# Retention with SiLU feed-forward on one core: two products moved into visits 7 and 9, with the order of loads, slices and read-backs around them

## The chip, the core and the metric

The kernel runs on one core of one Trainium2 chip. Its engines are TensorE (PE, with weight loads listed as PEld), VectorE (DVE), ScalarE (ACT), GpSimd (POOL) and SyncE (SP), which here issues the DMAs. The metric is the device time in microseconds: the kernel before took 631.07 us as the median of 6 runs (629.87 to 632.33).

## What is computed

```python
# q, k, v: (4, 8, 768, 64) float32        attention without softmax, one decay for each head
gamma = 1.0 - 2.0 ** (-5.0 - np.arange(H))
for t in range(S):
    state = gamma * state + einsum('bhd,bhe->bhde', k[:, :, t], v[:, :, t])
    y[:, :, t] = scale * einsum('bhd,bhde->bhe', q[:, :, t], state)
x = y.transpose(0, 2, 1, 3).reshape(3072, 512)
h = x @ w_in                               # w_in  (512, 2048)
g = h * (1.0 / (1.0 + np.exp(-h)))
out = g @ w_out                            # w_out (2048, 512)
```

The weights come as 64-bit numbers, so each slice of them has to be converted before it is used.

## The kernel before

**Units.** The sequence is cut into NC = 6 chunks of 128 steps. A unit is one chunk of one of the B = 4 batches; there are 24, numbered chunk by chunk, so units 0 to 3 make chunk 0 and units 4 to 7 chunk 1. For a unit, PE transposes k and q (`stage_t`, called T), multiplies k with v and k with q (`stage_s` and `stage_a`, the score step SC), and later forms the unit's output y (`stage_y`) in two halves: the masked scores and the products with the state of one half of the heads (YA), then those of the other half (YB). Between the two halves `fence` makes PE wait for a memset on POOL that waits for PE's last matmul of the first half. DVE multiplies the scores with the decay mask (`am`, L462), forms `mid` and the new state (L470, L474) and scales q (L395). ACT copies PSUM tiles out: kt and qt (L430), and the output y (`ys`, L531). Each y becomes three parts of x, high, low and third (`split_x`, called X: L544 on ACT, L547 and L550 on DVE).

**Weights.** w_in has NF = 16 slices of 128 columns. A slice is loaded by three DMAs (`load_w`), converted (`convert_steps`: L197 on ACT; L200, L203, L207, L210, L213 and L218 on DVE), and split in three parts (`split_steps`: L121 and L127 on ACT, L124 and L129 on DVE). There are two buffers (tag "wf") for slices as they come in; `convert_w(i)` asks for the load of slice i + 2, which has to wait until slice i has been read. `begin_w` does the conversion of the next slice, `end_w` its split. `take_w` does both behind a given product. The 16 slices of w_out are converted by `take_w` in the course of chunks 0 to 5, written to DRAM, and read back and split during chunk 5 (`get_w`, `w_out`, two ahead).

**Products.** `product_in(c, f)` is one product of the first feed-forward step: chunk c with slice f, 12 matmuls of 128 by 512. Eight of them go to a PSUM tile ha (parts 0 and 1) and four to hb (part 2). `close_in` copies ha (ACT L644), subtracts hb (DVE L648) and applies SiLU (ACT L652). The result g goes to DRAM (`put_g`), because the second step, g times w_out (L886), begins only after all 96 products. PSUM tiles for products and transposes rotate over three banks (`turn`).

**What sets the order.** PE's order is as written in the program. Up to `early_order.close()` (L793) the order of the other engines is as written too: it is a list of the steps T, K, SC, A, Q, YA, YB, X and W for units 0 to 5. After that the compiler's scheduler orders SP, ACT, DVE and POOL, within the bounds of `issue_after`, which puts instructions of an engine behind a given one on that engine (`taken_out` is the last subtraction L648, `masked` the last mask L462, `evac` the last copy of qt, `held` the last high part of x).

**Visits.** From unit 6 on the work is done in visits. `visit(m)` transposes unit m, does the score step of unit m - 1 and the output of unit m - 2, asks for loads of units m + 1 and m + 2, and then ends and begins slices. `halves(m)` is a visit that stops once, before the score step, so that a product can be placed there. With EARLY = 8, visits 6, 7, 8 and 9 come first; visit 8 holds product (0,2). Visits 10, 11 and 12 are taken in halves, with a product behind each half (`pairs`); visit 13 follows the last of the pairs. Then come groups of three products (`three`), and visits 14 to 25 are strewn among the later products (`at`). Chunk c = 1 can be multiplied only after visit 9, which finishes unit 7.

Begun slices before the change: `begin_w` runs in visits 6, 8, 10, 11, 12 and 13 (slices 2 to 7), and `end_w` in the next visit each time.

Of the kernel before, what the change touches and what calls it, by code (L numbers as in the profile page):

```python
# [13 lines left out]
FP32 = mybir.dt.float32  # L14
# [19 lines left out]
def kernel(  # L34
# [29 lines left out]
    B, H, S, D = q.shape  # L64
    DM, DF = moe_w_in.shape
# [15 lines left out]
    def pool(name, bufs, **kw):  # L81
        return ctx.enter_context(tc.tile_pool(name=name, bufs=bufs, **kw))
# [6 lines left out]
    one = pool("one", 1)  # L89
    hpool = pool("hpool", 3)  # L90
    stage = pool("stage", 2)
# [40 lines left out]
    def split_w(*of):  # L132
        steps = split_steps(*of)
        next(steps)
        yield
        list(steps)
# [4 lines left out]
    EARLY = 2 * B  # L141
# [79 lines left out]
    def convert_w(i):  # L221

        if i + W_AHEAD not in staged:
            load_w(i + W_AHEAD)
        out = []
        steps = convert_steps(i, out)
        for _ in range(6):
            next(steps, None)

        def rounded():  # L230
            list(steps)
            return out[0]

        return rounded
# [40 lines left out]
    def begin_w():  # L275

        i = taken[0]
        taken[0] += 1
        split = split_w(i, convert_w(i)(), "wi", scale, w_sb, True)
        next(split)  # L280
        half_split.append(split)
# [61 lines left out]
    behind_next, behind_copy, half_split = [], [], []  # L343
    taken_out, copied, masked, fenced = [], [], [], []
# [76 lines left out]
    def stage_t(n):  # L421

        for name, to, bufs, src, tp in (
                ("kt", kt, 2, kqv["k"][n], turn(f"kp_{n}")),
                ("qt", qt, 3, kqv["q"].pop(n), banks("q", f"qp_{n}", 1)[:, 0])):
            tp = tp.rearrange("p (a t) -> p a t", a=HP)
            for a in range(HP):
                nc.tensor.transpose(tp[:, a, :], src[:, 2 * a : 2 * a + 2, :], ident)
            to[n] = one.tile([128, HP, C], FP32, tag=name, name=f"{name}_{n}", bufs=bufs)
            evac[:] = [nc.scalar.copy(out=to[n], in_=tp).ins]  # L430

    def score_tile(n):
        u = banks("s", f"sc_{n}")
        sc, sums = (u[:, :, ts(i, 4 * D)].rearrange("p o (a t) -> p o a t", a=HP)
                    for i in range(2))
        return sc, sums

    def stage_s(n, sums):

        kf, vs = kqv["k"].pop(n), kqv["v"][n]  # L440
        for a in range(HP):
            for o in range(2 if units[n][0] < NC - 1 else 1):
                for j in range(2):
                    nc.tensor.matmul(sums[ts(j, D), o, a, :], lhsT=kf[ts(o, D), 2 * a + j, :],  # L444
                                     rhs=vs[ts(o, D), 2 * a + j, :], start=True, stop=True,
                                     skip_group_check=True)

    def stage_a(n, sc):

        ktn = kt.pop(n)  # L450
        for a in range(HP):
            for o in range(2):
                for j in range(2):
                    nc.tensor.matmul(sc[ts(o, D), j, a, :], lhsT=ktn[ts(j, D), a, ts(o, D)],  # L454
                                     rhs=qt[n][ts(j, D), a, ts(o, D)], start=True, stop=True,
                                     skip_group_check=True)
# [62 lines left out]
    def finish_y(n, yp):  # L519
        list(steps_y(n, yp))  # L520
# [60 lines left out]
    def visit(m):  # L581

        list(halves(m))

    def halves(m):

        first, mid, last = (0 <= m - i < len(units) for i in range(3))
        if first and m < FAR:
            stage_t(m)
        if last:  # L590
            scores, states_with, yp = stage_y(m - 2)
            scores()
            states_with(0)
        yield
        if mid:
            sc, sums = score_tile(m - 1)
            stage_s(m - 1, sums)
            stage_a(m - 1, sc)
            if 1 < m <= 3 * B + 1 and units[m - 1][1] == 0:
                next_chunk()  # L600

            with tc.issue_after(taken_out[0]) if m > 3 * B + 1 else ExitStack():
                finish_a(m - 1, sc, sums)
            scale_q(m - 1)
            if m > 3 * B + 1 and units[m - 1][1] == B - 1:

                behind_copy.append(next_chunk)
        if first and m < FAR:
            scale_k(m)
        if last:  # L610
            states_with(1)
            finish_y(m - 2, yp)

        if FAR <= m < len(units):
            with tc.issue_after(fenced[0]):
                part_t(m)
        for name in "kqv":
            for n in (m + 1, m + 2):
                if n >= EARLY and n == (m + 1 if name == "v" or n > FAR else m + 2):
                    load(name, n)  # L620
        if EARLY - 2 <= m < 3 * B + 2:
            with tc.issue_after(masked[0]):
                end_w()
                if m not in (EARLY - 1, EARLY + 1):
                    begin_w()


# [2 lines left out]
    def product_in(c, f):  # L630
        close_in(c, f, *multiply(c, f))
# [23 lines left out]
    def put_g(keep):  # L655
        while len(pending) > keep:
            c, f, g = pending.pop(0)
            nc.sync.dma_start(out=g_dram[c, f], in_=g)
# [14 lines left out]

    def get_w(f):
        if f < NF:
            t = stage.tile([128, DM], FP32, tag="wf", name=f"wr_{f}")
            nc.sync.dma_start(out=t, in_=wo_dram[f])
            w_got[f] = t

    def w_out(f):  # L680
        list(split_w(f, w_got.pop(f), "wo", 1.0, wo))
        get_w(f + 2)

    blocks = {}

    def split(n):
        if n >= len(order):
            return
        c, f = order[n]
        get(n + G_AHEAD)  # L690
        g = got.pop(n)
# [9 lines left out]
        ready[n] = t  # L701

    G_AHEAD = 4
    S_AHEAD = 3


# [5 lines left out]
    def SC(n):  # L712
        sa[n] = sc, sums = score_tile(n)
        stage_s(n, sums)
        stage_a(n, sc)
        asteps[n] = steps_a(n, sc, sums)

    def A(n):
        next(asteps[n], None)

    def YA(n):
        ys[n] = stage_y(n)
        ys[n][0]()
        ys[n][1](0)

    def YB(n):
        ys[n][1](1)
        ysteps[n] = steps_y(n, ys[n][2])

    def X(n):  # L730
        next(ysteps[n], None)
# [3 lines left out]
    def W(i, times=1):  # L735
        if i not in slices:
            slices[i] = early_slice(i)
        for _ in range(times):
            next(slices[i], None)
# [5 lines left out]
    K, Q = scale_k, scale_q  # L745
# [20 lines left out]
    YB(1), X(1), X(1)  # L766
    T(3), K(3)
    X(1), X(1)
    YA(2), SC(3)
    A(3), A(3), Q(3), A(3)  # L770
    YB(2), X(2), X(2)
    W(1), W(1)
    X(2), X(2)
    YA(3), YB(3), X(3), X(3)
    W(1)
# [18 lines left out]

    product_in(0, 1)
    put_g(1)
    visit(EARLY - 2)
    visit(EARLY - 1)
    eighth = halves(EARLY)
    next(eighth)  # L800
    product_in(0, 2)
    put_g(1)
    list(eighth)
    visit(EARLY + 1)
    half_visits = (x for m in range(EARLY + 2, 3 * B + 1) for x in chain(halves(m), (None,)))
    next(half_visits)

    half = NF // 2
    pairs = [(1, 0), (1, 1), (1, 2), (0, 3), (1, 3), (0, 4)]
    three = [(1, 4)] + [x for f in range(5, half) for x in ((0, f), (1, f), (2, f - 5))]  # L810
    rest = ([(2, f) for f in range(half - 5, half)] +
            [(c, f) for c in range(2) for f in range(half, NF - 4)])
    last = ([(c, f) for c in range(2) for f in range(NF - 4, NF)] +
# [8 lines left out]
    takes += [(4, f) for f in (3, 7, 11, 14)]  # L822
    takes += [(5, f) for f in (1, 3, 5)]
    behind = {x: lambda: next(half_visits) for x in pairs[:-1]}
    behind[0, 4] = lambda: [visit(3 * B + 1), behind_next.append(end_w)]
    at = ([(1, NF - 1)] + [(2, f) for f in range(NF - 7, NF - 2, 2)] +
          [(c, 4 * i + 1) for c in range(3, NC - 1) for i in range(B)])
    for i, x in enumerate(at):
# [9 lines left out]
    for n, (c, f) in enumerate(steps):  # L838
        if n - 2 in far:
            behind_next.append(lambda m=far[n - 2]: scale_k(m))  # L840
        if n - 3 in far:
            behind_copy.append(lambda m=far[n - 3]: [join_t(name, m) for name in "qk"])
        product_in(c, f)
        if (c, f) in takes:
            take_w(taken_out[0], n < len(pairs + three))
        put_g(1)
        behind.get((c, f), lambda: None)()
        if n - 1 in far:
            turn_t(far[n - 1])
        if c == NC - 1:  # L850
            if f == 0:
                get_w(0)
                get_w(1)
            if f < NF - 4:
                w_out(f)
            if f >= NF - 6:
                if f == NF - 6:
                    for n in range(G_AHEAD):
                        get(n)
                if f >= NF - S_AHEAD:  # L860
                    split(f - NF + S_AHEAD)
    put_g(0)

    for c in range(NC):
# [9 lines left out]
        for f in range(NF):  # L874
            n = c * NF + f
            split(n + S_AHEAD)
            if n < 4:
                w_out(NF - 4 + n)
            t = ready[n]
# [17 lines left out]
        for b in range(B):  # L897
            oa, ob = acc[b]
            o = one.tile([128, DM], FP32, tag=("kt", "qt")[b % 2], name=f"o_{c}_{b}",
                         bufs=(2, 3)[b % 2])  # L900
# [45 lines left out]
```

## Time and profile before

| | |
|---|---|
| median of 6 runs | 631.07 us (629.87 to 632.33) |
| the profiled execution | 631.8 us, its span 629.8 us |
| mean granted TensorE clock | 0.992 |
| PE busy | 606.1 us, 96% of the span |
| DVE busy | 422.7 us, 67% |
| ACT busy | 319.0 us, 51% |
| DMA | 107.31 MB, mean 170 GB/s |
| first matmul | at 4.29 us |
| product (1,0) begins | at 65.21 us |
| the second feed-forward step begins | at 362.72 us |

Times are counted from the first instruction of the profiled execution. A row of the time-ordered view gives the start, the time, the engine, the line, the operation with its tiles, and in brackets how long the engine had been idle and what ended that. A row of the waits view gives the waiting engine and line, what it waited for, the sum, the number and the longest. A busy time is a share of one engine alone; that an engine is busy doesn't say that the end depends on it.

### The profile page before, as it was taken

What the parts mean: (1) busy time and instruction counts of PE and PEld (TensorE: products, weight loads), DVE (VectorE), ACT (ScalarE), POOL (GpSimd) and SP (SyncE); (2) the same over time, 40 slices, a digit from 0 to 9 for tenths busy, and PEclk for the clock granted to TensorE, in tenths of its full rate; (3) what the DMA queues carried; (4) which work ended last, traced back from release to release, by engine and by line L of the source; (5) the groups of instructions that cost most, each with busy time, mean ns of one, the idle gap of its engine ahead of it and who ended that gap; (6) DMA issues with size and microseconds to landing.
All of it is one profiled execution on the core that took longest, in us unless ns stands there. A gap on an engine that the chain in (4) does not pass through costs nothing.

```text
span 629.8 us, 13488 instructions
## 1 busy us (share of the span) xinstructions
PE 606.1 (96%) x5384; PEld 498.3 (79%) x5384; DVE 422.7 (67%) x729; ACT 319.0 (51%) x611; POOL 22.6 (4%) x79
## 2 busy tenths in 40 slices
PE   5797999999999999999999999999999999999997
PEld 4675787888888888888887878888888888888886
DVE  4778798788979887777598885463645545554631
ACT  7578797666756566566567871221412221322311
POOL 3000000000000121111000000000000000000000
PEclk9799999999999999999999999999999999999999
DMA  9997687445578799998657764342433524442301
GB/s 189 214 228 179 164 242 234 151 153 181 161 218 235 203 265 245 239 248 243 240 195 234 221 191 134 103 160 72 148 120 93 175 70 131 134 120 81 134 1 67
DMA packets 137998, 107.31 MB, mean 170 GB/s; under 512 B 94800, under 2 KB 103248, under 8 KB 137936
## 3 DMA queue, kind: packets, MB, share of 16 engines
q1 hardware_dynamic: 135056, 101.21, 56.7%
q10 hardware_dynamic: 2880, 5.24, 2.2%
q8 instruction: 42, 0.69, 0.5%
q14 instruction: 20, 0.16, 0.1%
HBM read 66.06 MB, written 36.70 MB: 163 GB/s over the span
## 4 chain that ended last, share of the span: by engine, by line
PE 85%; DVE 5%; SPq 4%; DMA 3%; ACT 2%; issue 1%; DVEq 0%; POOLq 0%
PE ha L637 25%; PE o L886 20%; PE oa L886 14%; PE hb L637 12%; PE ob L886 7%; SPq L159 3%; PE y L493 3%; PE sc L444 1%; PE sc L454 1%; DMA kqv<-in_q_dram 1%; DMA wr<-wod 1%; DVE g L648 1%; DVE ca L213 1%; DMA wf<-in_moe_w_in_dram 1%; DVE cs L207 1%
## 5 line engine op out<-in xcount | busy, mean ns | idle before, releaser
L637 PE MATMUL ha<-xt,wi 128*128 128x512 f32 x768 | 194.8, 395 | 2.3 <-DVE g L648 1.5
L637 PEld LDWEIGHTS ha<-xt,wi 128*128 128x128 f32 x768 | 143.0, 189 | 34.9 <-DVE g L648 2.8
L886 PE MATMUL o<-wo,gs 128*128 128x512 f32 x564 | 143.2, 389 | 0.0
L886 PEld LDWEIGHTS o<-wo,gs 128*128 128x128 f32 x564 | 105.9, 188 | 21.9
L697 DVE TENSOR_TENSOR gs<-gr,gs 128x512 fp32r<-128x512 f32 x96 | 62.2, 686 | 88.5 <-ACT gs L695 88.5
L695 ACT ACTIVATE gs<-gr 128x512 fp32r<-128x512 f32 x96 | 53.5, 621 | 131.5 <-issue 130.8
L886 PE MATMUL oa<-wo,gs 128*128 128x512 f32 x376 | 115.9, 389 | 0.3 <-DVE g L648 0.3
L637 PE MATMUL hb<-xt,wi 128*128 128x512 f32 x384 | 103.0, 390 | 0.1
L648 DVE TENSOR_TENSOR g<-g,hb 128x512 f32<-128x512 f32 x96 | 65.7, 684 | 46.4 <-ACT g L644 28.4
L652 ACT ACTIVATE g<-g 128x512 f32<-128x512 f32 x96 | 60.5, 630 | 53.3 <-DVE g L648 53.2
L637 PEld LDWEIGHTS hb<-xt,wi 128*128 128x128 f32 x384 | 71.9, 188 | 15.8 <-DVE wi L129 0.6
L886 PEld LDWEIGHTS oa<-wo,gs 128*128 128x128 f32 x376 | 70.5, 188 | 15.2 <-DVE g L648 0.7
L886 PE MATMUL ob<-wo,gs 128*128 128x512 f32 x188 | 73.8, 393 | 0.3 <-ACT g L644 0.3
L644 ACT ACTIVATE g<-ha 128x512 f32<-128x512 f32 x96 | 56.8, 592 | 29.6 <-PE ha L637 20.9
L698 DVE SCALAR_TENSOR_TENSOR gs<-gs 128x512 fp32r<-128x512 f32 x96 | 62.1, 685 | 0.0
L886 PEld LDWEIGHTS ob<-wo,gs 128*128 128x128 f32 x188 | 35.3, 188 | 9.4 <-DVE o L904 1.6
L197 ACT ACTIVATE ca<-wf 128x512 f32<-128x512 f32 x32 | 21.4, 670 | 8.2 <-DVE cw L218 6.7
L462 DVE TENSOR_TENSOR am<-sc,decay 128x512 f32<-128x512 f32 x24 | 16.5, 688 | 11.2 <-PE sc L454 11.2
L213 DVE SCALAR_TENSOR_TENSOR ca<-wf,ca 128x512 f32<-128x512 uint32 x32 | 22.7, 710 | 0.4
L903 ACT ACTIVATE o<-o 128x512 f32<-128x512 f32 x10 | 6.0, 598 | 33.4 <-PE o L886 33.0
L207 DVE SCALAR_TENSOR_TENSOR cs<-ca,cs 128x512 uint32<-128x512 uint32 x32 | 22.1, 690 | 0.8
L493 PE MATMUL y<-qt,mid 64*64 64x64 f32 x384 | 21.0, 227 | 0.6 <-POOL token L365 0.6
(91 smaller groups left out, 566.3 us busy)
## 6 DMA issues: line engine op xcount, KB each, us to landing
gd<-g SPq DMA_DIRECT2D x96, 256.0 KB, 3.1
gr<-gd SPq DMA_DIRECT2D x96, 256.0 KB, 2.7
wf<-in_moe_w_out_dram SPq DMA_DIRECT2D x16, 512.0 KB, 4.2
out_dram<-o ACTq DMA_DIRECT2D x20, 256.0 KB, 2.1
wf<-in_moe_w_in_dram SPq DMA_DIRECT2D x16, 256.0 KB, 4.1
wf<-in_moe_w_in_dram SPq DMA_DIRECT2D x32, 128.0 KB, 3.9
kf<-in_k_dram SPq DMA_DIRECT2D x16, 256.0 KB, 5.1
qf<-in_q_dram SPq DMA_DIRECT2D x16, 256.0 KB, 4.6
```

The source lines that it names most:

```text
L197: nc.scalar.activation(out=a.bitcast(FP32), in_=hi.bitcast(FP32), func=AF.Abs, scale=65536.0)
L207: nc.vector.scalar_tensor_tensor(out=s, in0=a, scalar=3, in1=s, op0=ALU.logical_shift_left, op1=ALU.bitwise_or)
L213: nc.vector.scalar_tensor_tensor(out=p.bitcast(FP32), in0=lo, scalar=2.0 ** -52, in1=p.bitcast(FP32), op0=ALU.mult, op1=ALU.mult)
L493: i = nc.tensor.matmul(yp[ts(e, D), o, a, :], lhsT=lhsT, rhs=rhs, start=(e, o) not in started, stop=True, skip_group_check=True).ins
L637: nc.tensor.matmul(hb if i == 2 else ha, lhsT=w_sb[f][:, i, ts(kk, 128)], rhs=xt[c][:, i, kk, :], start=kk == 0 and i != 1, stop=kk == KIN ...
L644: copied[:] = [nc.scalar.activation(out=hs, in_=ha, func=AF.Copy, scale=ONE_E).ins]
L648: taken_out[:] = [nc.vector.tensor_tensor(out=hs, in0=hs, in1=hb, op=ALU.subtract).ins]
L652: nc.scalar.activation(out=hs, in_=hs, func=AF.Silu)
L695: nc.scalar.activation(out=t[:, 0, :], in_=g, func=AF.Copy, scale=HALF)
L697: nc.vector.tensor_tensor(out=t[:, 1, :], in0=g, in1=high, op=ALU.subtract)
L698: nc.vector.scalar_tensor_tensor(out=t[:, 2, :], in0=t[:, 1, :].bitcast(FP32), scalar=-1.0 / EPS, in1=high, op0=ALU.mult, op1=ALU.add)
L886: nc.tensor.matmul(o, lhsT=g, rhs=wo[f][:, i, :], start=f == 0 and i != 1, stop=f == NF - 1 and i != 0)
```

## The change

Four things are done. The early list puts the second half of unit 2's output, and the first step of X(2) (the copy of y), ahead of unit 3's score step. Visits 7 and 9 are taken in halves with products (0,2) and (0,3) inside; visit 8 has none, and `pairs` takes up (1,4) from the front of `three` where it has lost (0,3). The slices are begun sooner: slice 2 before visit 6, behind the subtraction of (0,1), and slices 3 to 7 in visits 7, 9, 10, 11 and 12. And the read-backs of w_out use the five buffers of tags kt and qt instead of the two of "wf", and run four ahead instead of two.

```diff
@@ visit
             with tc.issue_after(masked[0]):
                 end_w()
-                if m not in (EARLY - 1, EARLY + 1):
+                if m not in (EARLY - 2, EARLY, 3 * B + 1):
                     begin_w()
@@ get_w, w_out
-            t = stage.tile([128, DM], FP32, tag="wf", name=f"wr_{f}")
+            tag = "kqkqq"[f % 5]
+            t = one.tile([128, DM], FP32, tag=f"{tag}t", name=f"wr_{f}",
+                         bufs=2 if tag == "k" else 3)
...
-        get_w(f + 2)
+        get_w(f + W_READ)
...
+    W_READ = 4
@@ the early list
-    YA(2), SC(3)
-    A(3), A(3), Q(3), A(3)
-    YB(2), X(2), X(2)
-    W(1), W(1)
+    YA(2), YB(2), X(2)
+    SC(3), A(3), A(3), Q(3), A(3)
+    X(2), W(1), W(1)
     X(2), X(2)
@@ the visits
+    with tc.issue_after(taken_out[0]):
+        begin_w()
     visit(EARLY - 2)
-    visit(EARLY - 1)
-    eighth = halves(EARLY)
-    next(eighth)
-    product_in(0, 2)
-    put_g(1)
-    list(eighth)
-    visit(EARLY + 1)
+    for m, f in (EARLY - 1, 2), (EARLY, None), (EARLY + 1, 3):
+        parts = halves(m)
+        next(parts)
+        if f:
+            product_in(0, f)
+            put_g(1)
+        list(parts)
...
-    pairs = [(1, 0), (1, 1), (1, 2), (0, 3), (1, 3), (0, 4)]
-    three = [(1, 4)] + [x for f in range(5, half) for x in ((0, f), (1, f), (2, f - 5))]
+    pairs = [(1, 0), (1, 1), (1, 2), (1, 3), (0, 4), (1, 4)]
+    three = [x for f in range(5, half) for x in ((0, f), (1, f), (2, f - 5))]
...
-    behind[0, 4] = lambda: [visit(3 * B + 1), behind_next.append(end_w)]
+    behind[pairs[-1]] = lambda: [visit(3 * B + 1), behind_next.append(end_w)]
@@ chunk 5
-                get_w(0)
-                get_w(1)
+                for i in range(W_READ):
+                    get_w(i)
```

## The prediction

> **What bounds the kernel now.** I read the page first: parts 1 and 2.
>
> ```profile
> PE 606.1 (96%) x5384; PEld 498.3 (79%) x5384; DVE 422.7 (67%) x729; ACT 319.0 (51%) x611; POOL 22.6 (4%) x79
> ...
> PE   5797999999999999999999999999999999999997
> ```
>
> PE is idle for 629.8 - 606.1 = 23.7 us in all, and the change leaves PE's work alone. So it can only earn from idle time, or from work done at a low clock. The slices show where idle time is: in the first seven slices (to about 110 us), and hardly after. The second view is the engines' busy time by stage: visits 6 to 9 (39 to 65.2 us), the pairs of products (69.9 to 94), the step from pairs to threes (94 to 105).
>
> ```profile
> 39.00:65.20 26.20, 20.13 (x616) 16.58 (x616) 20.52 (x40) 22.62 (x61) 0.35 (x4) 1.00 0.79 196
> ...
> 69.90:94.00 24.10, 23.93 (x475) 19.80 (x468) 22.05 (x43) 20.94 (x51) 0.27 (x3) 1.00 0.78 217
> 94.00:105.00 11.00, 10.14 (x53) 7.40 (x45) 10.73 (x20) 8.69 (x21) 0.00 (x0) 1.00 0.81 230
> ```
>
> After the length the columns are PE, PEld, DVE, ACT, POOL, clock, DMA share, GB/s. In the visits PE has 6.07 us free, DVE 5.68, ACT only 3.58. In the pairs PE is full. At the step DVE is full (10.73 of 11.00) and PE loses 0.86. Third, who PE waits for from 36 to 105 us:
>
> ```profile
> PE y L493 <- issue: 1.6, 2, 1.5
> PE y L493 <- DVE qt L395: 1.5, 2, 0.7
> PE y L493 <- DVE am L462: 1.0, 1, 1.0
> PE ha L637 <- DVE g L648: 0.9, 2, 0.7
> PE ha L637 <- ACT wi L127: 0.8, 2, 0.6
> ```
>
> These are chains, not one engine: the scores of a unit go to DVE for the mask (am) and for the scaling of q (qt), and PE needs both for the unit's output. A product of 12 matmuls placed between is what PE could do meanwhile. Fourth, DVE in time order shows that it too waits there, before the mask of unit 5:
>
> ```profile
> 42.89 0.69 DVE L462 TENSOR_TENSOR am<-sc,decay 128x512 f32<-128x512 f32 x1 [1.94 <-PE sc L454]
> ```
>
> Last, the clock around unit 3, by stretches of 3.41 us:
>
> ```profile
> 18.79:22.20 3.41, 1.30 (x51) 1.15 (x54) 3.02 (x6) 2.55 (x5) 0.00 (x0) 1.00 0.69 180
> 22.20:25.61 3.41, 2.24 (x80) 2.05 (x72) 1.27 (x3) 0.65 (x2) 0.09 (x1) 0.50 0.96 205
> 25.61:29.03 3.42, 2.88 (x51) 2.57 (x52) 2.23 (x5) 1.99 (x4) 0.09 (x1) 0.50 1.13 228
> 29.03:32.44 3.41, 3.41 (x12) 2.92 (x12) 2.83 (x5) 2.87 (x8) 0.00 (x0) 0.50 0.97 227
> ```
>
> From 22.20 to 32.44 PE ran at half clock, after a stretch in which it was busy for 1.30 of 3.41 us (it waited for unit 3's q).
>
> **Part 1: unit 2's output ahead of unit 3's scores.** Before, unit 3's output waits 1.44 us and starts at 25.87, because the copy of unit 2's output (ACT L531) comes at 25.23, behind the mask and mid of unit 3. With YB(2) and X(2) first, that copy can run at about 23, under SC(3). The cost: the two halves of unit 2's output now follow each other, and the fence between them (a POOL memset) is bare; where it is bare in this stage PE waits 0.28 and 0.30. So SC(3) ends at about 24.5 instead of 24.2, the mask at 25.2, and unit 3's output starts at 25.2: 0.65 earlier, so product (0,0) starts at 29.3 instead of 29.95. No DMA moves in this part: SP issues only loads here, in unchanged order.
>
> [...] By the row alone the part is worth 0.65. [...] I take 0.3. Bounds: 0, and 1.3 if the clock rises one window earlier (below).
>
> **Part 2: products in visits 7 and 9.** Before, only visit 8 holds a product, (0,2), and pairs hold (0,3). Afterwards (0,2) stands in visit 7 and (0,3) in visit 9, visit 8 has none, and one product less is left behind the visits. A product takes 1.81 + 0.91 = 2.72 us (the chain of waits, 106.93 to 109.65).
>
> The budget for the same 26.2 us: PE 20.13 + 2.72 = 22.9; DVE 20.52 + 0.60 (one more subtraction, L648, start to start) = 21.1, or 24.0 if slice 4's conversion also falls before (1,0) (six operations, 2.9 start to start); ACT 22.62 + 0.5 + 0.6 (copy L644, silu L652) + 0.57 (L197) = 24.3. It fits, with ACT the tightest at 93%.
>
> The chain, by hand. Slice 2's conversion moves to right behind the subtraction of (0,1), DVE 40.9 to 43.8. Of these 2.9 us, 1.94 fill the wait shown above; the other 0.9 is queued ahead of unit 5's mask, which comes at 43.8 instead of 42.9. ACT's L197 moves from 43.75 into its 0.90 idle before 40.35, and the copy of unit 4's output comes about as much earlier; PE gets to unit 5's scores part at 44.5 (44.94 before), and through its states when q is scaled, 45.7. Slice 2's split (L121, L124, L127, L129: 0.6 each) follows unit 4's xh and ends near 48.0, against 54.2 before. So (0,2) starts at about 46 and ends at 49.4, with 0.9 of waits inside. SC(6) is queued behind it on PE: 49.4 instead of 45.69, and unit 6's mask 50.4 instead of 49.27. This is the new wait of the change; behind it stand unit 6's output and visit 8. Visit 8, now free of a product, catches up: unit 7's mask about 55.5 (57.01 before), since slice 3's conversion, 2.9, is in DVE's queue ahead of it. Then (0,3) from 57.6 to 61.6, again with about 1 us of waits for its slice, unit 8's mask 62.6 (62.55 before), and (1,0) starts at 64.8 to 65.6, where it starts at 65.21 before with a product less behind it. I take 0.4 later than before: gain 2.72 - 0.4 = 2.3. Bounds: 1.0 if ACT must keep its 3.58 us free (1.7 of added work lengthens the stage), 3.7 if the hand timeline is all cover; below nothing only by the rival further on.
>
> The 1.5 us "issue" wait, at 46.81 inside visit 7, falls with the product ahead of it into time that PE spends multiplying; I count no gain for it, because DVE was then busy to 51.7 anyway. SP: slice 4's load now waits for slice 2's conversion at 43 instead of 49 (SP's longest wait, 3.9 us). If it is queued ahead of unit 8's k and q loads, these land at about 50 instead of 45; unit 8 is transposed at about 50.7, so this costs nothing, but with little to spare. POOL only does fences.
>
> **Part 3: the step to threes.** With conversions begun one visit sooner, the last is done in visit 12 and visit 13 only ends one: 2.9 us less for DVE just before 94 to 105, where PE loses 0.86 behind DVE's subtractions. I take 0.8; bounds 0 and 1.1.
>
> **Part 4: w_out read back four ahead.** Before, the read-backs share two buffers with the incoming w_out slices: the first is issued at 328.92 although product (5,0) began at 318, and ten reads wait on SP for DVE L124, 12.6 us in all. PE feels little of it: 0.68 at 335.37 (DVE L648) and 0.27 + 0.34 at 365, where ACT had stood 0.48 for a read: 1.29 together. Five kt/qt buffers are free by then, the last visit lying in (4,13), and are free again before the first output tiles. The four reads at (5,0) put four issues of 0.32 ahead of one write of g on SP; a write later by 1.3 us is covered by three buffers at 2.72 us a product. I take 0.6; bounds -0.3 and 1.3.
>
> **Sum.** 0.3 + 2.3 + 0.8 + 0.6 = 4.0. The profiled execution took 631.8 (span 629.8 and 2.0 around it), so 627.8 there; it lies 0.7 above the median 631.07, so 627.1 for the median. From (1,0) on, PE is full, so nothing should give it back.
>
> **Rivals.**
> 1. DVE and ACT set the visits. The product gets in, but the visits grow by most of it: part 2 gives 0.5, part 3 0.4, the others 0.9 as above. For: ACT is 93% full in the budget. Against: the new work goes into waits that the trace shows. 631.07 - 1.8 = 629.3. Chance 0.17.
> 2. The clock falls in visit 8. [...] Half clock for one or two stretches around (0,3) costs 1 to 2.5: about 628.8. [...] Chance 0.13.
> 3. The clock rises one window sooner. The stretch 25.61 to 29.03 held 2.88 busy and did not raise it; without 0.26 of its wait it holds 3.1. From 5.13 to 8.55 PE was busy 3.3, and its matmuls were fast from then. If it rises at 29.03, part 1 gives 1.3: 626.1. Chance 0.15.
> 4. Slower: (0,2) stops PE in visit 7. If the queues of DVE and ACT put slice 2's work behind visit 6's, as they do now, it is ready at 54.2, and SC(6) with everything behind it stands until (0,2) ends at 55.7 instead of 49.4. That costs 6.3 against 4.0: 633.4. It decides for slower from slice 2 landing 4 us behind my 48.0. Against: the conversion is written ahead of visit 6 and tied to the subtraction of (0,1). Chance 0.1.
>
> The forecast itself: 0.45.
>
> **Numbers.** About 0.2% (1.3 us) is what a measurement of this kernel can tell from no change: faster is below 629.8. Forecast, rival 3, most of rivals 2 and 1 lie there: 0.77. Within: 0.13. Slower: 0.10. Range 624.9 (the upper bounds of two parts together) to 630.6 (rival 1 with parts 3 and 4 at their low bounds); rival 4 stays outside.
>
> **What would show it.** Right: (0,2) starts near 46 and (0,3) near 57.6; (1,0) near 65; DVE's 1.94 wait filled; PE busy about 23 of 26.2 in the visits; no wait of 0.7 for L648 near 98 or 335; copy L531 of unit 2 near 23; the clock up at 32.4. Wrong: PE waiting over 2 us for L127 in visit 7 (rival 4), a half clock near 56 (rival 2), (1,0) past 67 (rival 1), or new PE waits in the pairs.

## The result and the profile after

The changed kernel takes 627.3 us (median of 21 runs, 625.77 to 630.84) against 631.26 us before (42 runs). The ratio is 0.994, with a 95% interval of 0.9926 to 0.9954, so it is faster by 2.9 to 4.7 us, 3.8 in the middle. The forecast was 627.1. The profiled execution took 626.11 us, its span 624.3. Page of the changed kernel, parts 1 and 2:

```profile
PE 606.0 (97%) x5384; PEld 497.5 (80%) x5384; DVE 422.4 (68%) x729; ACT 317.4 (51%) x611; POOL 22.1 (4%) x79
...
PE   6888999999999999999999999999999999999997
...
PEclk9999999999999999999999999999999999999999
```

PE's work is the same, and the early slices are fuller. But the last row shows a trap: in this execution the clock never dropped after the start, while the profiled execution of before ran at half clock from 22.20 to 32.44 us. The two spans therefore differ by 5.5 us, more than the medians (4.0), and the early stage can't be compared between them. What can be compared are stretches in which both ran at full clock. Who PE waited for from 36 to 105 us, after:

```profile
PE y L493 <- DVE am L462: 1.4, 2, 0.8
PE ha L637 <- ACT wi L127: 1.2, 2, 0.6
PE sc L454 <- issue: 1.1, 1, 1.1
PE y L493 <- DVE qt L395: 0.7, 1, 0.7
PE hb L637 <- ACT g L644: 0.5, 1, 0.5
PE ha L637 <- DVE g L648: 0.4, 1, 0.4
```

The waits did not vanish: these lines sum to 5.3 us, those of before to 7.1 (5.8 in the five shown there, 1.3 in three shorter ones). What changed is what PE gets done between them. The stretch from unit 6's transposes to product (1,0), in the order length, PE, PEld, DVE, ACT, POOL, clock, DMA; first before, then after:

```profile
39.99:65.21 25.22, 19.15 (x613) 15.81 (x611) 20.02 (x39) 22.18 (x60) 0.35 (x4) 1.00 0.78 192
```

```profile
36.90:63.57 26.67, 22.04 (x625) 17.63 (x623) 22.00 (x42) 23.25 (x61) 0.35 (x4) 1.00 0.88 212
```

It holds 12 matmuls more (x625 to x613), one product of 2.72 us by the prediction's row, and is 1.45 longer: 1.27 gained. DVE in time order shows slice 2's conversion right behind the subtraction of (0,1), and unit 5's mask behind it without a wait, where 1.94 stood before:

```profile
37.17 0.69 DVE L648 TENSOR_TENSOR g<-g,hb 128x512 f32<-128x512 f32 x1 [0.75 <-PE kp L428]
37.77 0.42 DVE L200 TENSOR_SCALAR cs<-wf 128x512 uint32<-128x512 uint32 x1
...
40.48 0.69 DVE L218 TENSOR_TENSOR cs<-cs,ca 128x512 f32<-128x512 f32 x1
41.09 0.68 DVE L462 TENSOR_TENSOR am<-sc,decay 128x512 f32<-128x512 f32 x1
```

Two more stretches can be cut in every trace: from (1,0) to (2,0), which holds the step to threes, and from the last bare fence of the products (312.24 before, 307.28 after) to the end, which holds the read-backs and the second feed-forward step. PE's waits at the step to threes, where (2,0) begins with the last row of each view (103.92 before, 98.94 after):

```profile
100.58 2.11 PE L637 MATMUL ha<-xt,wi 128*128 128x512 f32 x8 [0.68 <-DVE g L648]
103.92 2.11 PE L637 MATMUL ha<-xt,wi 128*128 128x512 f32 x8 [0.18 <-DVE g L648]
```

```profile
97.37 1.20 PE L637 MATMUL hb<-xt,wi 128*128 128x512 f32 x4 [0.50 <-ACT g L644]
98.94 2.11 PE L637 MATMUL ha<-xt,wi 128*128 128x512 f32 x8 [0.37 <-DVE g L648]
```

All stretches are differences of starts in PE's time-ordered view.

| kernel | median us | unit 6 to (1,0) | (1,0) to (2,0) | last fence to end |
|---|---|---|---|---|
| before | 631.26 | 25.22 | 38.71 | 317.56 |
| changed | 627.3 | 26.67 | 35.37 | 317.02 |
| order alone | 631.41 | 25.21 | 38.72 | 317.62 |
| visits and slices alone | 628.02 | 26.65 | 35.08 | 317.75 |
| read-backs alone | 630.24 | 26.18 * | 40.10 * | 316.97 |
| slices sooner alone | 630.06 | 27.69 * | 37.88 | 318.63 |
| slice 2 late | 635.12 | 32.85 * | 35.08 | 316.96 |
| split not held | 626.94 | 26.40 | 35.11 | 317.41 |
| read-backs two ahead | 627.67 | 26.66 | 35.17 | 316.95 |
| no scaling of k | 625.76 | 26.68 | 35.09 | 317.11 |
| no scaling of q | 625.05 | 25.18 | 35.05 | 317.09 |
| useless work in visits 7, 8 | 633.71 | 25.68 | 39.22 | 318.06 |
| work in the wait for q | 626.95 | 26.67 | 35.08 | 317.04 |
| split and two ahead | 625.7 | 26.40 | 35.09 | 316.98 |

A star marks an execution whose clock was halved inside the stretch. Kernels with (0,3) inside the visits have one product of 2.72 more in the first stretch and one less in the second. Between them, from (2,0) to that fence, both kernels took the same: 208.32 before and 208.34 after.

Each execution in the experiments, and each of the changed kernel's, is also recorded with its mean granted clock. A least-squares fit over these, with one offset for each kernel and one common slope on (1 - clock) x 630 us, gives 0.57 us of time for each us of clock lost and a scatter of 0.73. One execution of before, at 681.48 us with a clock of 0.852, was slow as no other and is left out. Differences at equal clock below are differences of these offsets, with their 95% interval: the changed kernel is 2.65 +- 0.34 faster than before. The runs were taken in several series, and the kernel before alone lies 0.15 above its common offset in one of them and 0.16 and 0.20 below it in two others, so a difference between kernels of different series is uncertain by some 0.3 more.

### The profile page after: what moved, and what is told of

The parts are those of the page before. It is cut to its first block, busy times and chain, and to the rows that moved or that the text cites. A ratio compares the mean times of both kernels' runs of the same rounds, so it can differ in the third digit from the quotient of the medians.

```text
span 624.3 us, 13508 instructions
## 1 busy us (share of the span) xinstructions
PE 606.0 (97%) x5384; PEld 497.5 (80%) x5384; DVE 422.4 (68%) x729; ACT 317.4 (51%) x611; POOL 22.1 (4%) x79
## 4 chain that ended last, share of the span: by engine, by line
PE 89%; DVE 7%; issue 1%; ACT 1%; DMA 1%; POOL 0%; DVEq 0%; POOLq 0%
PE ha L637 26%; PE o L890 20%; PE oa L890 14%; PE hb L637 13%; PE ob L890 7%; PE y L493 4%; PE sc L444 2%; PE sc L454 2%; PE kp L428 1%; PE qp L428 1%; DVE am L462 1%; DVE cs L207 1%; DMA wf<-in_moe_w_out_dram 1%; DVE ca L213 1%; DVE wol L124 0%
## 5 line engine op out<-in xcount | busy, mean ns | idle before, releaser
L648 DVE TENSOR_TENSOR g<-g,hb 128x512 f32<-128x512 f32 x96 | 65.7, 684 | 49.9 <-ACT g L644 29.2
L644 ACT ACTIVATE g<-ha 128x512 f32<-128x512 f32 x96 | 56.9, 593 | 32.9 <-PE ha L637 19.0
L462 DVE TENSOR_TENSOR am<-sc,decay 128x512 f32<-128x512 f32 x24 | 16.5, 687 | 6.4 <-PE sc L454 6.2
```

The costliest lines, as they stand in the source:

```text
L462: mask = nc.vector.tensor_tensor(out=am[n], in0=sc, in1=decay, op=ALU.mult).ins
L644: copied[:] = [nc.scalar.activation(out=hs, in_=ha, func=AF.Copy, scale=ONE_E).ins]
L648: taken_out[:] = [nc.vector.tensor_tensor(out=hs, in0=hs, in1=hb, op=ALU.subtract).ins]
```

## The experiments

**Part 1 alone.**

```diff
-    YA(2), SC(3)
-    A(3), A(3), Q(3), A(3)
-    YB(2), X(2), X(2)
-    W(1), W(1)
+    YA(2), YB(2), X(2)
+    SC(3), A(3), A(3), Q(3), A(3)
+    X(2), W(1), W(1)
```

> Only part 1: unit 2's second half and its copy ahead of unit 3's scores; all else as before. Theory A (read from the two traces): the profiled pair differs by 3.1 us up to visit 6, more than the 0.3 that the prediction gave part 1, but most of that is the half clock, which fell in one execution and not in the other; the order itself is worth 0.3 to 1.3: 630.0 to 631.0. Rival B: the order is the largest part of the gain, 2 us or more: under 629.3. Both expect the copy of unit 2's output near 23 us, no wait of 1.4 us for it, and everything from visit 6 to the end as long as before.

Measured: 631.41 us (14 runs), ratio 1.0004 (0.9984 to 1.0025); at equal clock 0.24 +- 0.41 faster. Its profiled execution also ran at half clock in the stretches 22.20 to 32.44, as before's did, so the two can be laid side by side. Time-ordered views of this kernel, of ACT, DVE and PE:

```profile
23.08 0.58 ACT L531 COPY ys<-y 128x512 f32<-128x512 f32 x1 [1.55 <-PE y L493]
```

```profile
24.82 0.69 DVE L462 TENSOR_TENSOR am<-sc,decay 128x512 f32<-128x512 f32 x1 [2.80 <-PE sc L454]
```

```profile
25.66 1.13 PE L493 MATMUL y<-am,kqv 64*64 64x64 f32 x32 [0.92 <-DVE am L462]
...
29.75 1.63 PE L637 MATMUL ha<-xt,wi 128*128 128x512 f32 x3
```

The copy comes at 23.08 as foreseen, and unit 3's output waits 0.92 instead of 1.44. But the scores end later. From the first state products of unit 2 to the mask it is 3.16 us (21.66 to 24.82) against 2.23 before (22.00 to 24.23): at half clock the bare fence and the second half cost 0.9. A head start of 0.34 hides a part of that: the load of unit 3's q stopped PE for 0.85 in this execution, not for 2.11. Unit 3's output and product (0,0) start 0.2 sooner (29.95 before); at unit 6 0.07 of it is left (39.92 against 39.99). In this pair the order is worth nothing.

At full clock it is worth more. From the first half of unit 2's output to that of unit 3 it is 4.02 us in the old order (slices sooner alone, 21.24 to 25.26) and 3.51 in the new one (the changed kernel, 21.29 to 24.80), 0.5 gained. Up to unit 6 the old order took 15.97 there, and the four executions of the new one that were at full clock 15.61 to 16.02. So the order gives 0 to 0.4 in single executions. Over all runs its effect can't be told from none, nor from the predicted 0.3. Rival B, the order as the main part, falls.

**Parts 2 and 3 alone**: the changed kernel with the early list and the read-backs as before.

> Parts 2 and 3 alone: products in visits 7 and 9, slices begun sooner, the early list and the read-backs as before. Theory A (the traces): from unit 6's transposes to product (1,0) 26.7 us instead of 25.2 with one product of 2.72 more, so 1.3 gained; from (1,0) to (2,0) 0.6 gained; 1.9 in all: 629.4. The prediction's own sizes give 2.3 + 0.8 = 3.1: 628.2. Rival B (the early order is the main part) would leave under 1: over 630.3.

Measured: 628.02 us (14 runs), ratio 0.9946 (0.9928 to 0.9964), at equal clock 2.13 +- 0.41 faster. Rival B falls. The stretches give what theory A expected, 25.22 + 2.72 - 26.65 = 1.3 and 38.71 - 2.72 - 35.08 = 0.9, but the median moved by 2.9, nearer the prediction's 3.1. The difference is mostly clock: the mean granted clock of these runs is 0.9966, before's 0.9946, which the fit prices at 0.7.

**Part 4 alone** (`W_READ = 4` is set as in the change, and chunk 5 begins with four reads).

```diff
-            t = stage.tile([128, DM], FP32, tag="wf", name=f"wr_{f}")
+            tag = "kqkqq"[f % 5]
+            t = one.tile([128, DM], FP32, tag=f"{tag}t", name=f"wr_{f}",
+                         bufs=2 if tag == "k" else 3)
-        get_w(f + 2)
+        get_w(f + W_READ)
...
+    W_READ = 4
```

> Part 4 alone: w_out read back four ahead in the kt and qt buffers. Theory A (the traces): chunk 5's products take 0.7 longer, the second feed-forward step 1.2 less; 0.5 gained: 630.8, hard to tell from no change in time, but both halves show in the trace. Rival: the 0.7 longer stems from the other parts (another position of visits against the read-backs), then this kernel gains 1.2: 630.1.

Measured: 630.24 us (22 runs), ratio 0.9983 (0.9969 to 0.9996); at equal clock 0.59 +- 0.34 faster, and the stretch from the last fence to the end 0.59 shorter. PE's waits in it besides the fence's own, this kernel's only one and then the three of before:

```profile
341.86 2.11 PE L637 MATMUL ha<-xt,wi 128*128 128x512 f32 x8 [0.40 <-DVE g L648]
```

```profile
335.37 2.12 PE L637 MATMUL ha<-xt,wi 128*128 128x512 f32 x8 [0.68 <-DVE g L648]
...
364.96 0.50 PE L886 MATMUL ob<-wo,gs 128*128 128x512 f32 x1 [0.27 <-ACT g L644]
365.80 0.73 PE L886 MATMUL oa<-wo,gs 128*128 128x512 f32 x2 [0.34 <-DVE g L648]
```

From fence to second step it is 51.13 against 50.48, 0.65 longer, and the rest is 1.24 shorter: theory A in both halves. More split work falls into the first part (DVE does 75 operations there instead of 72, ACT 68 instead of 64), and the second step then starts without a wait. The 0.65 itself is in no wait of the view: PE's busy time there is 50.66 against 49.80, and why is left open.

**Slices sooner alone**: slices begun as in the change, (0,2) left in visit 8 and (0,3) in the pairs.

```diff
-                if m not in (EARLY - 1, EARLY + 1):
+                if m not in (EARLY - 2, EARLY, 3 * B + 1):
                     begin_w()
...
+    with tc.issue_after(taken_out[0]):
+        begin_w()
     visit(EARLY - 2)
```

> The slices begun sooner, as in the change, but the products where they were: (0,2) in visit 8, (0,3) in pairs. Theory A: the sooner slices are what relieves DVE at the step from pairs to threes, so (1,0) to (2,0) gets about 0.6 shorter, and visits 6 to 9 change little, for they wait on chains and (0,2)'s wait for its slice (0.6) goes: 630.1. Rival: the sooner slices crowd DVE and ACT in visits 6 to 9, which get about 1 us longer, and the gain of the change is all in the placing of the products: 631.7.

Measured: 630.06 us (14 runs), ratio 0.9988 (0.9971 to 1.0006), at equal clock 0.81 +- 0.41 faster. (1,0) to (2,0) is 0.83 shorter: theory A on the step to threes. For the visits themselves this execution can't tell, because the clock dropped in them. Its stretches of 3.4 us there:

```profile
44.70:48.10 3.40, 0.72 (x11) 0.51 (x7) 3.24 (x7) 3.08 (x9) 0.00 (x0) 1.00 0.81 184
48.10:51.50 3.40, 3.02 (x57) 2.26 (x54) 1.77 (x4) 2.57 (x8) 0.00 (x0) 0.52 1.09 257
51.50:54.90 3.40, 3.40 (x8) 2.72 (x9) 2.27 (x4) 1.04 (x5) 0.09 (x1) 0.50 0.91 203
```

With no product in visit 7, PE was busy 0.72 of 3.40 us (its longest wait was 2.1 us, for issue), and most of product (0,2) then ran at half clock. So the rival, visits about 1 us longer, is neither shown nor excluded for this kernel.

**Slice 2 late**: the changed kernel, with slice 2 begun in visit 6 behind the mask and split just ahead of (0,2).

```diff
-    with tc.issue_after(taken_out[0]):
-        begin_w()
     visit(EARLY - 2)
...
         next(parts)
+        if f == 2:
+            with tc.issue_after(masked[0]):
+                end_w()
```

> The changed kernel, but slice 2 is begun in visit 6 behind unit 5's mask, as in the kernel before, and split in visit 7 just ahead of product (0,2), which keeps its place. Theory A (the prediction's fourth rival): PE stands at (0,2) until slice 2 lands, with unit 6's scores queued behind it, so visits 6 to 9 get 4 to 6 us longer than in the changed kernel: 631.3 to 633.3. Rival B: DVE has so much room in visit 7 that the slice lands about 2 us later and visit 8 catches up: under 629.

Measured: 635.12 us (9 runs), ratio 1.007 (1.0047 to 1.0094). PE, time-ordered:

```profile
49.30 3.78 PE L637 MATMUL ha<-xt,wi 128*128 128x512 f32 x8 [4.93 <-ACT wi L121]
```

PE stands 4.93 us for the slice, then multiplies at half clock (0.50 in the rows of one us from 49 to 54; 3.78 for eight matmuls, where those of the views above take 2.1). The visits are 6.2 longer than in the changed kernel, and the mean clock of the runs is 0.9896; at equal clock the kernel is 4.8 us behind the changed one (2.18 +- 0.52 slower than before, plus 2.65). Theory A holds, and the clock adds to it.

**Split not held**: the changed kernel, L121 of slices 2 and 3 bound behind the copy of qt instead of x.

```diff
-        split = split_w(i, convert_w(i)(), "wi", scale, w_sb, True)
+        split = split_w(i, convert_w(i)(), "wi", scale, w_sb, i > 3)
```

> The changed kernel, with the splits of slices 2 and 3 bound behind the last copy of qt instead of behind the high part of x, so that ACT may do L121 before the high part of unit 4's and 6's x. Theory A: PE's two waits for L127 inside (0,2) and (0,3), 0.60 and 0.62, end and the time falls by 0.6 to 1.2 to about 626.4. Rival B: the x parts come later by the same amount and (1,0), or the next mask, waits for them: 627.3, no change.

Measured: 626.94 us (8 runs), ratio to before 0.9941 (0.9918 to 0.9964); visits 0.27 shorter than in the changed kernel. The waits for L127 went from 1.2 to 0.8 only. The gain is below what these runs can tell; neither theory is decided.

**Read-backs two ahead**: the changed kernel with `W_READ = 2`.

> The changed kernel, with w_out read back two ahead instead of four, still in the kt and qt buffers. Theory A: it is the buffers of its own that matter, since two ahead is 5.4 us of products and a read lands in 2.8: as the changed kernel, 627.3. Rival B: the depth matters, and it falls back to the kernel with parts 2 and 3 alone: 628.0 or more, with PE waits near 365 us back in the trace.

Measured: 627.67 us (12 runs), ratio to before 0.9946 (0.9925 to 0.9967); last fence to end 316.95, and besides the fence's own PE's only wait there is the same one of 0.4 for L648. Theory A: buffers of their own make the gain of part 4, and the depth makes none that shows.

**Useless work in visits 7 and 8**, in the kernel before.

```diff
             states_with(1)
+            if m in (7, 8):
+                fill = turn(f"fill_{m}")
+                for _ in range(12):
+                    nc.tensor.transpose(fill[:, :128], ident, ident)
```

> The kernel before, with 12 transposes of 128 by 128 that nobody reads behind unit 5's and unit 6's output, in visits 7 and 8: useless work of about 1.4 us each in PE's idle time. Theory A (the clock): part of the gain of the change is that PE no longer stands idle in visits 7 and 8 long enough for its clock to be halved there, as it was from 48 to 55 us with slices sooner alone and from 50 to 53 us with read-backs alone. Then the useless work makes the kernel before faster: mean granted clock up from 0.9944 to 0.996, time down by 0.6 to 630.3. Rival B: the clock is lost around unit 3 alone and falls as often as before; the transposes only cost, 631 to 632.

Measured: 633.71 us (13 runs), ratio 1.0043 (1.0025 to 1.0062). The mean clock was 0.9960, where before, measured beside it, had 0.9943 (29 runs); the gap is 1.6 of its standard errors, so it agrees with theory A without showing it. At equal clock the kernel is 2.86 +- 0.42 slower: the visits took 0.46 more, the step 0.51, the stretch from (2,0) to the last fence 1.34 (PE stood 1.03 for issue at 209) and the rest 0.50. Most of that lies far behind the added work. The two added tiles also take turns in the rotation of PSUM banks, so every later tile of that rotation has another bank, and the program has 49 instructions more. The time is rival B's, but what the clock alone is worth this kernel can't tell.

**What lengthens the visits.** Two kernels take work off one engine each. First the changed kernel without the scaling of k for three units, on ACT:

> The changed kernel without the scaling of k (L379 on ACT) for units 6, 7 and 8, so these units' sums are left unscaled: about 6 us less for ACT in visits 6 to 8, nothing else removed. From unit 6's transposes to (1,0) the changed kernel takes 26.67 us, 1.45 more than before instead of the 0.4 that the prediction had. Theory A: chains over PE and DVE set the visits, and ACT only stands beside: 26.3 to 26.7, time about 627. Rival B (the prediction's first rival): ACT's queue is what lengthens them: 25.6 or less, time 626.2.

Measured: visits 26.68 us, as in the changed kernel; 625.76 us (7 runs), ratio to before 0.9938 (0.9916 to 0.996). ACT's queue does not set the visits, though ACT is busy 18.68 us from 36 to 64 us instead of 24.18; rival B falls. The median is lower mostly by clock (mean 0.9981); at equal clock 0.6 remain against the changed kernel, no more than the fit's uncertainty for so few runs. Then without the scaling of q for four units, on DVE:

> The changed kernel without the scaling of q (L395 on DVE) for units 5 to 8, so these units' state products are left unscaled: four operations of 0.6 us less on DVE, each of them in the chain from a mask to the states of that unit. Theory A (DVE's queue and the chain through it): the stretch from unit 6's transposes to (1,0) falls from 26.67 by 1.2 or more, to 25.5 or less, and the time to about 626. Rival B (ACT): it stays above 26.3.

Measured: visits 25.18 us, 1.49 less; 625.05 us (4 runs), ratio 0.9918 (0.9891 to 0.9945). Theory A holds against ACT: the path leads through DVE. The chain of waits of the changed kernel shows it, in pieces of start, length, what:

```profile
48.22 0.69 DVE am L462
...
50.17 0.34 DVE cs L200
50.52 0.60 DVE xt L547
51.11 0.34 DVE ca L203
51.45 0.60 DVE xt L550
52.05 0.61 DVE cs L207
52.69 0.44 DVE ca L210
...
53.15 0.69 DVE ca L213
53.84 0.60 DVE am L462
```

From unit 6's mask to unit 7's, which DVE's own rows put at 53.76, DVE doesn't pause, and slice 3's conversion lies ahead of the mask that PE waits for. But it is not there that the kernel without the scaling gains. Its masks (L464 is L462 there):

```profile
47.71 0.69 DVE L464 TENSOR_TENSOR am<-sc,decay 128x512 f32<-128x512 f32 x1 [0.38 <-PE sc L456]
53.26 0.69 DVE L464 TENSOR_TENSOR am<-sc,decay 128x512 f32<-128x512 f32 x1
```

They are 5.55 us apart, against 5.54 in the changed kernel: the scheduler put one more operation of the conversion (L218) ahead of the second mask, where the scaling had made room. Of the 1.49, counted from unit 6's transposes, 0.3 is gained up to the first mask and 1.0 between the second and product (0,3). There the changed kernel has L218, mid and the scaling behind the mask, and PE waits for the last of them:

```profile
56.03 0.27 PE L493 MATMUL y<-qt,state 64*64 64x64 f32 x1 [0.74 <-DVE qt L395]
```

So what this kernel shows is that the chain from a mask through the scaling of q to the state products is on the path. That the conversion ahead of unit 7's mask is on it too is read from the chain alone; no run moved only that.

**Work in the wait for unit 3's q**, in the changed kernel: the same 12 transposes between k and q of unit 3.

> The changed kernel with 12 transposes that nobody reads between unit 3's k and q, where PE waits for q in some executions. Theory A (the clock): the half clock around unit 3 starts from this wait, so the work keeps the clock up: mean granted clock from 0.9961 to 0.998 or more, but the transposes cost up to 1.3 us where PE doesn't wait: 627 to 628. Rival B: the clock falls as often as before, since it is the stretch after unit 3 that decides: 0.996 and 628 or more.

Measured: 626.95 us (5 runs, 626.31 to 627.06), ratio to before 0.9944 (0.9923 to 0.9965), mean clock 0.9982. That is theory A's number, but the profiled execution was at half clock from 25.7 to 29.1 all the same, and three other kernels with the new visits reach 0.998 in 4 to 7 runs of the same series, in which before had 0.9958. What starts the half clock near unit 3 stays open.

**Both small edits together**: split not held and two ahead.

> The changed kernel with both earlier edits together: splits of slices 2 and 3 not held behind x, and w_out read back two ahead. Theory A: the first saves 0.4 and the second nothing: 626.9. Rival B: both were chance, and it comes out at the changed kernel's 627.3 to 627.7.

Measured: 625.7 us (6 runs, 625.24 to 626.57), ratio to before 0.9932 (0.9913 to 0.9951). It is the fastest complete version, at equal clock 1.1 +- 0.66 us ahead of the changed kernel by the fit; but the intervals of the two ratios overlap, the two kernels are from different series, and the stretches show 0.27 of it in the visits and 0.28 at the step, so part of it may be chance.

## Why the prediction was right, point by point

The forecast 627.1 met 627.3, and the sum of 4.0 met 3.8 (2.9 to 4.7). That the two numbers agree so closely is luck: the terms by themselves came to about 2.4, and what was in no term made up for the rest.

**Part 1, predicted 0.3, measured 0.24 +- 0.41.** The copy came at 23.08, as foreseen, and the clock was up near 32.5 with the order alone, at 32.44 before. No run shows the 0.3 of the sum as what is left of 0.65. What the runs showed in its place: at half clock product (0,0) started 0.2 sooner and 0.07 was left at unit 6; at full clock, where the plain sum gave 0.65, 0.5 was gained up to unit 3's output and 0 to 0.4 up to unit 6. Mis-sized in the plain sum is the bare fence with the second half, 0.3 there and 0.9 in the trace at half clock. Rival 3 did not occur (its window is one stretch of 3.41 us): the stretch 25.61 to 29.03 held 3.09 us of PE work with the order alone, and the clock still did not rise.

**Part 2, predicted 2.3, measured 1.27** by the trace, and the same within 0.03 in five kernels with the new visits (26.65 to 26.68). The mechanism is the predicted one. Seen from unit 6's transposes, which are 3.09 earlier after the change: (0,2) starts at 46.2 (46 predicted), SC(6) at 50.1 (49.4), unit 6's mask at 51.3 (50.4), unit 7's at 56.9 (55.5), (0,3) at 59.5 (57.6), (1,0) at 66.7 (64.8 to 65.6). So the term that was mis-sized is "I take 0.4 later than before": it was 1.45. The hand timeline lost 0.7 by the end of the product, which started 0.2 later and took 3.8 instead of 3.4, then 0.2 up to the mask, 0.4 between the two masks and 0.6 up to (0,3); from there to (1,0) it had 0.85 too much. The budget named ACT as the tightest engine. That was the wrong engine: taking 5.5 us off ACT changed nothing, taking four operations of 0.6 us off DVE gave 1.49.

**Part 3, predicted 0.8, measured 0.62** (0.83 to 0.91 in the kernels with slices or visits alone). DVE no longer has a conversion at the step, as predicted, and its wait of 0.68 is gone. A new wait for ACT's copy (L644), 0.50, stands beside the 0.37 that is left; in four other kernels with the new visits it is 0.16 to 0.24 and the stretch 0.2 to 0.3 shorter. The prediction had no term for ACT there. **Part 4, predicted 0.6, measured 0.54 to 0.61**; only it is the separate buffers that do it, not the four reads ahead.

These terms sum to 1.3 + 0.6 + 0.5 = 2.4, in agreement with 2.65 +- 0.34 at equal clock. **The rest was not in the sum, and a part of it is clock.** The mean granted clock was 0.9946 before (94 runs) and 0.9961 after (22, one more than the median counts); 0.0015 x 630 x 0.57 = 0.5 us. With it the terms and the fit reach 2.9 to 3.2, at the lower end of the measured interval. What is missing to 3.8 is not explained: the 42 executions of before that it is counted from have no clock on record, and their median, 631.26, lies 0.5 above that of the 94 (630.8).

**The rivals.** Rival 2 did not come true. It feared a half clock in visit 8 once it holds no product. In the eight profiled executions with the new visits and slice 2 in time, none lost clock in visits 7 to 9. Among the kernels with the old visits, two of five executions lost clock at 48 to 55 us. And over all runs of the five complete kernels with the new visits and nothing added the mean granted clock is 0.9966 (62 runs), over those of the four with the old visits 0.9943 (144). So the new visits go with a higher clock. That it is the product in visit 7 that does it, by filling a gap, is argued from the place: no run shows it alone. PE's idle time was there, too. In visit 8 and the start of (0,3) the changed kernel has a stretch of 3.41 us with PE busy 2.05, and the kernel with visits and slices alone one with 1.84, both without a drop, while elsewhere 1.81 to 2.14 came before one (last section). Rival 4 was priced right: it foresaw 2.3 us slower than before, and with slice 2 begun late it was 2.18 +- 0.52 at equal clock, with a wait of 4.93 at the place named; the clock lost in the wait brought the median to 635.12. Rival 1 lies between: the visits did grow by half of the product, but through DVE.

## What to carry to other kernels

A product placed in a chain's gap was worth its length less what it delayed (2.72 less 1.45 here, 1.27); add up the chain operation by operation, with every engine whose queue lies in it, since a share of busy time named the wrong engine here (ACT at 93% in the budget, where 5.5 us less of it changed nothing). Its operands must be finished before the engine gets there: the same change with one slice begun later stood 4.93 us for it and is slower than before. A kernel that leaves out work shows that the work is on the path, but not where: look up in its trace what took the free place. And compare two profiled executions only where their clocks agree; a fit over all runs with the granted clock as a variable brought the uncertainty of a kernel's difference to 0.3 to 0.7 us.

## What the runs showed of the hardware

**Busy time alone doesn't tell when the clock drops or rises.** Ten of the fourteen traces show drops of the clock before 58 us, twelve in all. In rows of one us, which place a change to within 0.02, the clock was back after 3.40 to 3.42 us in six of them, after 6.82 to 6.84 in three (slices sooner alone, slice 2 late, useless work) and after 10.24 in three (before, order alone, two ahead): 3.41 us, or two or three times that. Cut into stretches of 3.41 us at these times, PE was busy just before a drop 0.75 us (slices sooner alone, to 48.21), 1.30 (before, to 22.20) and 1.81 (order alone, to 22.32), but also 2.12 (two ahead, to 22.42) and 2.14 (slice 2 late, to 27.57). Stretches with 1.78 (useless work, to 14.45), 1.82 (order alone, to 15.49) and 2.05 (changed, to 58.70) passed without one. So none of these stretches before a drop was without work, and the two groups overlap. One row of each, the first with the drop behind it (two ahead), the second without (changed):

```profile
19.01:22.42 3.41, 2.12 (x54) 1.64 (x58) 2.80 (x6) 2.45 (x5) 0.09 (x1) 1.00 0.92 232
```

```profile
55.29:58.70 3.41, 2.05 (x22) 1.43 (x23) 3.41 (x7) 3.22 (x10) 0.09 (x1) 1.00 0.96 274
```

The same holds for the rise: 3.30 of 3.41 us of small matmuls (before, to 8.55) and 3.05 (work in the wait for q, to 8.64) raised it, while 3.13 (changed, to 14.33) and the 3.09 above did not. What counts besides stays open.

**The granted clock in the rows is not to be trusted at the start.** It reads 1.00 there, while four transposes of the changed kernel took 1.09 us at 4.28, 1.11 at 15.65 and 0.66 at 19.57. When the clock first rises differs by execution: four transposes near 11 us took 0.65 or 0.66 us in six of the fourteen traces, before among them, and 1.11 in eight. A load for unit 3 then stopped PE for 0.44 to 2.11 us in four of the six, and in none of the eight.

**PE's waits "for issue" ended soon after packets of the instruction queue.** In the first 320 us before has three of them, of 1.48, 0.60 and 0.17 us, and the changed kernel one of 1.13. All four end 2.36 to 2.67 us after a packet of 16 KB of the queue of instructions (q8) began: in before, packets at 45.84, 57.90 and 91.34 and ends at 48.51, 60.55 and 93.70; in the changed kernel, 49.84 and 52.43. Whether PE's next instructions came late there, and why such waits move when matmuls are added, no run shows.
